# Attention outputs finished two steps later, weight preparation by a table of steps, a fourth word tile, one low part on VectorE

## The chip, the cores and the metric

The kernel runs on one core of a Trainium2 chip. The metric is the device time of one execution in microseconds (us), the median of several runs. Engines are named as in the profile: PE is TensorE (PEld its weight loads), DVE is VectorE, ACT is ScalarE, POOL is GpSimd, SP is SyncE, which issues DMAs.

## The reference

Three blocks follow one another, all on float32 data with 2 batches, 8 heads, 768 positions, head size 64 (model width 512).

```
# 1. attention inside clusters
q_assign = argmax(q_n @ c_n.T); k_assign = argmax(k_n @ c_n.T)       # 16 centroids per head
scores = where(q_assign == k_assign, (q @ k.T) / sqrt(D), -1e9)
attn = exp(scores - max); attn = attn / (sum(attn) + 1e-9)
x = attn @ v                                                          # heads side by side: (2, 768, 512)
# 2. mixing over positions, then a feed-forward block of width 2048
u = x + (xt @ U @ V).transpose;  y = u + relu(u @ w_ch1) @ w_ch2
# 3. gated block of width 1024
h = relu(y @ w_in); conv_out = 3-tap convolution of h along the positions
out = (h * sigmoid(conv_out)) @ w_out
```

## The kernel before, in words

Attention runs as 96 steps n, one for each head and each 128 of its 768 query rows, six to a head. Two heads make a pair, so a pair has twelve steps s = 0 to 11, and there are eight pairs (0 to 7). The whole program is written out by hand (`manual_schedule`): each engine executes its instructions in the order in which the code issues them, and waits only for data and for buffers. So the order of the calls in `step(n)` is the order of the work.

A step n issues, in this order: on PE the scores of step n + 2 (`s_mm`, tile `sc`, L356 and L367); in some steps other PE work; then six transposes of the exponentials of step n (`t_mm`, tile `tr`, L393, two tiles of three transposes). The copies of `tr` out of PSUM (tile `pt`, L400) follow one step later: the first half on ACT, the second on DVE. ACT forms the exponentials (L384), DVE scales the scores and takes their extreme (`s_max`, L373). When six rows of a head are transposed, `pv_mm` (L409) multiplies by the values in two lots of six matmuls, in steps of rest 2 and 5 of `g, r = divmod(n - 7, 6)`; these are s = 3, 9 and s = 6, 0. After the second lot ACT copies the sum (`asb`, L418); `fin_t` (L425, tile `at`) transposes it on PE in three matmuls, and `fin_x` takes the reciprocal of the sums (L431) and multiplies (L434, tile `x`) on DVE.

The PSUM pool `ps_t` has three tiles for `tr`, `at`, `sim`, `simw`, `oht`, `mt`, `mx`, so a transpose has to wait until one of the older three has been read out.

Beside this stand three kinds of work, put into fixed steps:
- the cluster masks of the next pair: `sims_wide` (s = 0), `sims_turn` (s = 2, tile `sim`, L224), five DVE operations ending in L249 (tile `oh`), `onehot_t` (tile `oht`, L263) and its rows on ACT (L269);
- the low parts of the next pair's operands, `split_ops` (L119, L120 on POOL, tile `ab`), in `prep(n)`;
- the preparation of weights. They come as 64-bit words and are joined to float32 by a chain of stages: DMA (`job_dma`, tile `raw`), `job_base` (ACT, L462), `job_low` (DVE, L470), `job_join` (DVE, L475), `job_put` and `job_more` (cast on ACT, low part on POOL). During attention `pump()` moves one job by one stage in every odd step; from step 86 on `begin()` and `tick()` take over, and the jobs still under way go on from there, one stage in a tick. The words stand in tiles `wx`, of which there are three (`word_tile`).

The mixing of a batch (`mix_t`, tile `mt`, L650; `mix_x`, tile `mx`, L670) is queued at s = 8 of the pair behind the batch's last and taken up in steps 3, 4, 9, 10 that issue no `fin_t`.

The feed-forward block (about 250 to 510 us of the span) forms seven products in place of eight with tiles pa to pd (L838), and sums (`acc`, L898 to L900) that DVE adds to `xa` (L902). The gated block has its own units (c, b, f): PE forms `g` (L930 to L932), ACT and DVE the convolution and gate (L933, L949, L953, L957, L959), and `split(f)` the high part (ACT, L963) and the low part (POOL, L964) of the product, which PE reads for `po` (L982).

Of the kernel before, what the change touches and what calls it, by code (L numbers as in the profile page):

```python
# [19 lines left out]
I32 = mybir.dt.int32  # L20
# [6 lines left out]
P = 128  # L27
# [6 lines left out]
def tile_kernel(ctx: ExitStack, tc: tile.TileContext, qk, vv, cen, u_w, v_w, w1, w2, win, wout, conv, out):  # L34
    nc = tc.nc
    B, H, D, _, S = qk.shape
    NC = cen.shape[0] // H
    NP = H // 2
# [18 lines left out]
    wst = right.enter_context(tc.tile_pool(name="wst", bufs=1, side="right"))  # L57
# [144 lines left out]
    ohst = {}  # L202
# [48 lines left out]
    def behind_onehot(b, p):  # L251

        seen = a_oh.tile([P, 1], BF16, tag="seen", name="seen")
        nc.gpsimd.tensor_copy(seen, kept[b, p][:, 0, 0:1])

    kept = {}

# [163 lines left out]
    def fin_t(g):  # L421
        asb = st.pop(("asb", g))
        pt = ps_t.tile([P, NK, 2, D], F32, tag="t", name="at")
        for t in range(NK):
            nc.tensor.transpose(pt[:, t].rearrange("p a d -> p (a d)"), asb[:, t * P:(t + 1) * P], identf)  # L425
        st["at", g] = pt
# [23 lines left out]
    def job_dma(j):  # L450
        raw_ = wst.tile([P, UN, 2], I32, tag="raw", name="raw", bufs=2)
        for p0, src in j["src"]:
            pn, n = src.shape
            nc.sync.dma_start(out=raw_[p0:p0 + pn, 0:n], in_=src.bitcast(I32).rearrange("p (a b) -> p a b", b=2))
        j["raw"] = raw_[0:p0 + pn, 0:n]
# [6 lines left out]
        nc.scalar.activation(j["b"], j["raw"][:, :, 1].bitcast(F32), AF.Prelu, scale=float(2.0 ** -112), alpha=float(2.0 ** 32))  # L462

    def word_tile():
        return wst.tile([P, UN], I32, tag="wx", name="wx", bufs=3)

    def job_low(j):
        pn, n, _ = j["raw"].shape
# [17 lines left out]
    def job_more(j, count=3):  # L486
        for f in j["left"][:count]:
            f()
        del j["left"][:count]
        if not j["left"]:  # L490
            del full[:j.get("held", 1)]

    THIN = {0: job_dma, 2: job_base, 3: job_low, 4: job_join, 5: job_put, 6: job_more, 8: job_more}

    def pump():

        for j in list(fly):
            j["at"] += 1
            if j["at"] in THIN:
                THIN[j["at"]](j)  # L500
            if j.get("left") == []:
                fly.remove(j)
        if jobs and not fly:
            j = jobs.pop(0)
            j["at"] = 0
            job_dma(j)
            fly.append(j)


    words, puts = [], []  # L510
# [11 lines left out]
    def tick():  # L522
        clock[0] += 1
        for j in fly:
            words.extend([lambda f=THIN[k], j=j: f(j) for k in sorted(THIN) if k > j["at"] and k < 6])
        fly.clear()
        if puts and puts[0][0] in opened:
            puts.pop(0)[1]()
        if words:
            words.pop(0)()  # L530
        elif begun and clock[0] - begun[0]["at"] > 4 and len(full) < 3:
            j = begun[0]
            job_base(j)

            def low():
                job_low(j)
                begun.pop(0)
                begin()

            def last():  # L540
                job_join(j)
                full.append(j)
                x = j["x"].bitcast(F32)
                steps = j["steps"](x) if "steps" in j else [lambda: j["put"](x)]
                for i, f in enumerate(steps):
                    puts.append((j["slot"], lambda f=f, i=i: (f(), full.pop(0) if i >= len(steps) - j["held"] else None)))

            words.extend([low, lambda: None, last])
# [138 lines left out]
    def prep(n):  # L687

        pair, s = divmod(n, 2 * NT)
        nxt = pair + 1  # L690
        if nxt < B * NP:
            b, p = divmod(nxt, NP)
            for part, at in enumerate(ONEHOT_AT[nxt == 1]):
                if s == at:
                    sims_onehot(b, p, part)
            if s == 1 and nxt == 2:
                load_ops(b, p, 0)
            if s == (1, 3)[nxt < 3]:
                split_ops(b, p, 0, nc.gpsimd)
            if s == (3, 1)[nxt == 1]:  # L700
                load_ops(b, p, 1)
            if s == 7:
                behind_onehot(b, p)
                split_ops(b, p, 1, nc.gpsimd)
        if s == RAW_AT[pair == 0] and pair + 2 < B * NP:
            load_raw(*divmod(pair + 2, NP))
        if s == V_AT[pair == 0] and nxt < B * NP:
            load_v(*divmod(nxt, NP))
        if s == 10 and 0 < pair < B * NP - 2:
            load_ops(*divmod(pair + 2, NP), 0)  # L710
        if n >= NQ - 10:
            begin()
            tick()
        elif n % 2 == 1 and n > 1:
            pump()


    PLAN = ({2: (0, 1, 2), 5: (3, 4, 5)}, NT - 1), ({0: (0, 1, 2), 1: (3, 4, 5)}, 1)
# [5 lines left out]
    def step(n):  # L724
        pair, s = divmod(n, 2 * NT)
        mix = None
        if s == 8 and pair > 0 and n < NQ:
            b, p = divmod(pair - 1, NP)
            if p == NP - 1:
                mixing.append(mix_t(b))  # L730
                mix_rest(b)
        if n == 0:
            sims_wide(0, 1)
            warm(7)
        if n + 2 < NQ:
            s_mm(n + 2)
        ahead = divmod(pair + 1, NP)
        wide = 0 <= n < NQ and 1 < pair + 1 < B * NP
        rows = 0 <= n < NQ and pair + 1 < B * NP and s == ROWS_AT[pair == 0]
        turn = 0 <= n < NQ and pair + 1 < B * NP and s == TURN_AT[pair == 0]  # L740
        if rows:
            onehot_t(*ahead)

        g, r = divmod(n - NT - 1, NT)
        ks, last = PLAN[g == NHEAD - 1]
        if 0 <= g < NHEAD:
            for k in ks.get(r, ()):
                pv_mm(g, k)
        done = g - 1 if r == 0 else g if g == NHEAD - 1 and r == last + 1 else -1
        if 0 <= done < NHEAD - (r == 0):  # L750
            fin_t(done)
        elif mixing and (s in MIX_AT or pair == B * NP - 1):
            mix = mixing.pop(0)
            got = mix[0]()
        if s == SIM_AT and wide:
            sims_wide(*ahead)
        if turn:
            sims_turn(*ahead)
        if 0 <= n < NQ:
            t_mm(n)  # L760
        soon = n + 1 >= NQ - 1
        if soon and n + 1 < NQ:
            s_exp(n + 1)
        if 0 <= n - 1 < NQ:
            for i in range(2):
                t_out(n - 1, i)
        if 0 <= n + 1 < NQ and not soon:
            s_exp(n + 1)
        if rows:
            onehot_rows(*ahead)  # L770
        if (s == SIM_AT and wide) or n == 0:
            sims_copy(*ahead)
        if n == -1:
            split_first(1, "q")
            split_ops(0, 0, 1, nc.gpsimd)
            load_ops(0, 1, 0)
        if n + 2 < NQ:
            s_max(n + 2)
        if 0 <= g < NHEAD and r == 0:
            sm = st["sum", g]  # L780
            nc.gpsimd.tensor_scalar(out=sm, in0=sm, scalar1=1e-9, scalar2=None, op0=ALU.add)
        if 0 <= g < NHEAD and r == last:
            fin_a(g)
        if 0 <= done < NHEAD - (r == 0):
            fin_x(done)
        if mix:
            mix[1](got)
        if 0 <= n < NQ:
            prep(n)
# [146 lines left out]
    def gate(c, b):  # L936

        h = hs[c, b]
        i = made[0] * 4
        made[0] = (made[0] + 1) % (len(spare_tiles) // 4)  # L940
        own = [x.rearrange("p k s -> p (k s)") for x in spare_tiles[i:i + 4]]
        hs[c, b] = [own[0:2], own[2:4]]
        cv = {}

        def conv(f, t):
            w = cw[:, FPC * c + f]
            x = cv[f, t] = ps_a.tile([P, DM], F32, tag="abcd"[2 * f + t], name="cv")[:, 0:HS]
            a, z = t * HS, (t + 1) * HS
            nc.scalar.activation(x, h[f][:, a:z], AF.Identity, scale=w[:, 1:2])  # L949
            for k, d in ((0, -1), (2, 1)):  # L950
                lo, hi = max(a, -d), min(z, S - d)
                o = x[:, lo - a:hi - a]
                nc.vector.scalar_tensor_tensor(out=o, in0=h[f][:, lo + d:hi + d], scalar=w[:, k:k + 1], in1=o, op0=ALU.mult, op1=ALU.add)  # L953

        def close(f, t):
            x = cv.pop((f, t))
            nc.scalar.activation(x, x, AF.Sigmoid)  # L957
            o = h[f][:, t * HS:(t + 1) * HS]
            nc.vector.tensor_mul(o, o, x)  # L959

        def split(f):
            gh, gl = hs[c, b][f]
            nc.scalar.copy(gh, h[f])  # L963
            nc.gpsimd.tensor_sub(gl, h[f], gh)  # L964

        todo = [(conv, 0, 0), (conv, 0, 1), (conv, 1, 0), (close, 0, 0), (conv, 1, 1), (close, 0, 1), (close, 1, 0), (close, 1, 1), (split, 0), (split, 1)]
        for part, *at in todo:
            part(*at)
            yield
# [292 lines left out]
```

## Time and profile before

| | |
|---|---|
| median of 3 runs | 640.44 us (640.26 to 640.55) |
| the profiled execution's own time | 640.48 us |
| its span, first to last instruction | 638.7 us |
| granted TensorE clock | 1.000 |
| PE busy | 629.0 us (98%) |
| DVE busy | 422.9 us (66%) |
| ACT busy | 370.2 us (58%) |
| POOL busy | 314.6 us (49%) |
| chain that ended last: PE | 88% |
| chain: DVE, ACT, POOL | 3%, 3%, 2% |

The span lies inside the execution's own time; 1.8 us lie around it. Busy time of PE counts a matmul from its start to its modelled end. A matmul that stands alone or is held back is drawn longer than one in a full stream, so a high busy share does not say that PE was never held up; the starts of successive groups say more.

### The profile page before, as it was taken

The page shows a single profiled execution, that of the slowest core. Times are in us where ns is not written, and L with a number is a line of the kernel's source. Part 1 is how long each engine was busy: PE and PEld are TensorE (multiplying, and loading weights), DVE is VectorE, ACT ScalarE, POOL GpSimd, SP SyncE. Part 2 cuts the span into 40 slices and gives each one's busy share as a digit, 9 for nine tenths or more (in the row PEclk, how much of TensorE's full clock was granted, in tenths as well). Part 3 has the DMA queues.
Part 4 walks back from the last instruction along what each step waited for, and adds up shares of the span by engine and source line. Part 5 has one row for each costly group of instructions (what it writes and reads, how often), then busy time and mean ns, then how long its engine had stood idle before and what let it go on. Part 6 is the DMA issues. An engine that isn't in the chain of part 4 may idle for free.

```text
span 638.7 us, 10486 instructions
## 1 busy us (share of the span) xinstructions
PE 629.0 (98%) x3850; PEld 548.1 (86%) x3850; DVE 422.9 (66%) x833; ACT 370.2 (58%) x752; POOL 314.6 (49%) x320
## 2 busy tenths in 40 slices
PE   8999999999999999999999999999999999999997
PEld 5767777766777767999999999999999998889986
DVE  6968788686868684586765666666666468641762
ACT  5967777776777674647363434343354498655730
POOL 4835445256346622878655545463355455413330
PEclk9999999999999999999999999999999999999999
DMA  7696764836445110112321221121112211200022
GB/s 192 139 210 152 142 164 85 182 74 170 81 114 123 60 56 29 35 39 94 107 93 66 90 77 66 67 67 67 66 47 75 79 34 67 66 1 2 4 96 99
DMA packets 17860, 55.50 MB, mean 87 GB/s; under 512 B 3120, under 2 KB 3760, under 8 KB 17808
## 3 DMA queue, kind: packets, MB, share of 16 engines
q1 hardware_dynamic: 14208, 40.08, 20.7%
q0 software_dynamic: 3600, 14.75, 11.2%
q8 instruction: 30, 0.49, 0.3%
q14 instruction: 22, 0.18, 0.1%
HBM read 50.19 MB, written 3.15 MB: 84 GB/s over the span
## 4 chain that ended last, share of the span: by engine, by line
PE 88%; DVE 3%; ACT 3%; POOL 2%; issue 2%; DMA 1%; ACTq 0%; DVEq 0%; POOLq 0%
PE po L982 10%; PE pv L409 10%; PE tr L393 9%; PE acc L898 7%; PE acc L900 7%; PE acc L899 7%; PE pd L838 5%; PE pa L838 5%; PE pb L838 5%; PE sc L367 5%; PE sc L356 5%; PE pc L838 2%; PE g L931 2%; PE g L930 2%; PE g L932 2%
## 5 line engine op out<-in xcount | busy, mean ns | idle before, releaser
L384 ACT ACTIVATE e<-e,nb 128x768 f32<-128x768 f32 x96 | 90.5, 943 | 20.7 <-DVE e L373 20.4
L373 DVE TENSOR_SCALAR_CACHE_REDUCE e<-sc 128x768 f32<-128x768 f32 x96 | 91.3, 952 | 8.3 <-PE sc L367 7.1
L902 DVE TENSOR_TENSOR xa<-acc,xa 128x384 f32<-128x384 f32 x128 | 70.2, 555 | 39.1 <-PE acc L900 39.1
L898 PE MATMUL acc<-r,vh 128*128 128x384 f32 x256 | 86.0, 336 | 0.4 <-DVE xa L902 0.4
L900 PE MATMUL acc<-r,vl 128*128 128x384 f32 x256 | 85.6, 334 | 0.0
L899 PE MATMUL acc<-r,vh 128*128 128x384 f32 x256 | 85.5, 334 | 0.0
L393 PE MATMUL tr<-identf,e 128*128 128x128 f32 x576 | 82.8, 277 | 2.3 <-DVE pt L400 1.7
L393 PEld LDWEIGHTS tr<-identf,e 128*128 128x128 f32 x576 | 64.9, 140 | 23.4 <-issue 8.7
L400 DVE COPY pt<-tr 128x384 f32<-128x384 f32 x93 | 51.4, 552 | 35.3 <-PE tr L393 34.9
L409 PE MATMUL pv<-pt,rv 128*64 128x384 f32 x384 | 69.3, 494 | 0.0
L601 POOL TENSOR_TENSOR vl<-wx,vh 128x512 fp32r<-128x512 f32 x24 | 30.8, 1299 | 63.4 <-ACT vh L600 63.4
L356 PE MATMUL sc<-ab 128*128 128x384 f32 x192 | 57.1, 378 | 0.4 <-DVE ab L192 0.3
L400 ACT COPY pt<-tr 128x384 f32<-128x384 f32 x99 | 47.2, 481 | 16.5 <-PE tr L393 16.1
L953 DVE SCALAR_TENSOR_TENSOR cv<-h,cw,cv 128x383 f32<-128x383 f32 (+1 forms) x64 | 38.2, 620 | 27.5 <-ACT cv L949 26.4
L409 PEld LDWEIGHTS pv<-pt,rv 128*64 128x64 f32 x384 | 26.2, 136 | 28.1 <-issue 24.8
L367 PE MATMUL sc<-cd 80*128 80x384 f32 x192 | 49.4, 339 | 0.0
L898 PEld LDWEIGHTS acc<-r,vh 128*128 128x128 f32 x256 | 48.0, 188 | 1.5 <-DVE xa L902 1.3
L899 PEld LDWEIGHTS acc<-r,vh 128*128 128x128 f32 x256 | 48.1, 188 | 0.0
L900 PEld LDWEIGHTS acc<-r,vl 128*128 128x128 f32 x256 | 48.0, 188 | 0.0
L475 DVE SCALAR_TENSOR_TENSOR wx<-wb,wy 128x512 int32<-128x512 int32 (+1 forms) x42 | 28.1, 669 | 22.8 <-POOL vl L601 12.4
L881 POOL TENSOR_TENSOR r<-q,r 128x384 fp32r<-128x384 f32 x16 | 16.2, 1015 | 49.9 <-ACT r L880 49.9
L575 POOL TENSOR_TENSOR wl<-wx,wh 128x512 fp32r<-128x512 f32 (+1 forms) x32 | 36.3, 1155 | 6.7 <-DVE oh L249 4.3
(242 smaller groups left out, 1532.3 us busy)
## 6 DMA issues: line engine op xcount, KB each, us to landing
raw<-in_w_dram SPq DMA_DIRECT2D x32, 512.0 KB, 3.6
cd<-in_qk_dram POOLq DMA_DIRECT2D x15, 384.0 KB, 4.2
ab<-in_qk_dram POOLq DMA_DIRECT2D x15, 384.0 KB, 5.4
raw<-in_win_dram SPq DMA_DIRECT2D x8, 512.0 KB, 3.6
raw<-in_wout_dram SPq DMA_DIRECT2D x8, 512.0 KB, 3.5
rv<-in_vv_dram SPq DMA_DIRECT2D x8, 384.0 KB, 3.4
out_dram<-xa SPq DMA_DIRECT2D x12, 256.0 KB, 2.0
ab<-in_qk_dram POOLq DMA_DIRECT2D x15, 192.0 KB, 5.5
```

The lines of the kernel that those rows point to most:

```text
L356: nc.tensor.matmul(ps[:, f, 0:HS], ab[:, 0, c0:c0 + P], ab[:, 1, f * HS:(f + 1) * HS], start=True, stop=False)
L367: nc.tensor.matmul(ps[:, f, 0:HS], cd[0:80, 0, c0:c0 + P], cd[0:80, 1, f * HS:(f + 1) * HS], start=False, stop=True)
L373: nc.vector.tensor_scalar(out=e, in0=ps[:, :, 0:HS], scalar1=-SCALE, scalar2=3e38, op0=ALU.mult, op1=ALU.min, accum_out=nb,)
L384: nc.scalar.activation(e, e, AF.Exp, scale=-1.0, bias=nb, accum_out=st["sum", n // NT][:, n % NT:n % NT + 1])
L393: nc.tensor.transpose(pt[:, k, :], e[:, i, k * P:(k + 1) * P], identf)
L400: (nc.scalar.copy if i == 0 or n in (2, 3, 4) else nc.vector.tensor_copy)(to, st.pop(("t", n, i)))
L409: nc.tensor.matmul(acc[i * D:(i + 1) * D], vts[b, h // 2][:, h % 2, k], pt[:, k, i * NK:(i + 1) * NK].rearrange("p a b -> p (a b)"), start ...
L838: nc.tensor.matmul(o, l[:, k, w], r[:, k], start=first and not more, stop=last, skip_group_check=more)
L898: nc.tensor.matmul(acc, wh[:, f, ds_], r[:, 0], start=f == t, stop=False)
L899: nc.tensor.matmul(acc, wh[:, f, ds_], r[:, 1], start=False, stop=False)
L900: nc.tensor.matmul(acc, wl[:, f, ds_], r[:, 0], start=False, stop=f != t)
L902: nc.vector.tensor_add(o, acc, o)
```

## The change

Four things change.

1. `fin_t` and `fin_x` of a head move from the step of rest 0 (s = 1 and 7) to that of rest 2 (s = 3 and 9). `fin_t` stands there ahead of the first lot of `pv_mm`. The last head keeps its own place. The mixing is queued at s = 10 rather than 8 and may share a step with `fin_t`.
2. `pump(s)` is called in every step and follows the table PARTS: DMA at s = 4, base at 9, low at 11, join at 0, put at 3, further parts at 5 and 8. A job so takes about a pair's twelve steps. `tick()` starts at step 87 rather than 86, and a job that is under way hands over what is left of its parts too.
3. There are four word tiles rather than three. In the first pair, the splits of the second pair's first head wait for that pair's mask: `behind_onehot` issues a one-column copy of `oh` on POOL (tile `seen`) ahead of them, at s = 5 rather than 3.
4. The low part of one unit of the gated block, (c, b, f) = (1, 0, 0), is formed by DVE rather than POOL (L964).

```diff
@@ -251,7 +251,7 @@
     def behind_onehot(b, p):
 
         seen = a_oh.tile([P, 1], BF16, tag="seen", name="seen")
-        nc.gpsimd.tensor_copy(seen, kept[b, p][:, 0, 0:1])
+        nc.gpsimd.tensor_copy(seen, (kept.get((b, p)) or ohst[b, p]["oh"])[:, 0, 0:1])
 
     kept = {}
 
@@ -462,7 +462,7 @@
         nc.scalar.activation(j["b"], j["raw"][:, :, 1].bitcast(F32), AF.Prelu, scale=float(2.0 ** -112), alpha=float(2.0 ** 32))
 
     def word_tile():
-        return wst.tile([P, UN], I32, tag="wx", name="wx", bufs=3)
+        return wst.tile([P, UN], I32, tag="wx", name="wx", bufs=4)
 
     def job_low(j):
         pn, n, _ = j["raw"].shape
@@ -492,19 +492,21 @@
 
     THIN = {0: job_dma, 2: job_base, 3: job_low, 4: job_join, 5: job_put, 6: job_more, 8: job_more}
 
-    def pump():
-
+
+    PARTS = {4: 0, 9: 2, 11: 3, 0: 4, 3: 5, 5: 6, 8: 8}
+    order = sorted(THIN)
+
+    def pump(s):
+        if s in PARTS and PARTS[s] == 0 and jobs:
+            fly.append(jobs.pop(0))
+            fly[-1]["at"] = -1
         for j in list(fly):
-            j["at"] += 1
-            if j["at"] in THIN:
-                THIN[j["at"]](j)
-            if j.get("left") == []:
+            k = order[order.index(j["at"]) + 1] if j["at"] >= 0 else 0
+            if PARTS.get(s) == k:
+                j["at"] = k
+                THIN[k](j)
+            if j.get("left") == [] or j["at"] == order[-1]:
                 fly.remove(j)
-        if jobs and not fly:
-            j = jobs.pop(0)
-            j["at"] = 0
-            job_dma(j)
-            fly.append(j)
 
 
     words, puts = [], []
@@ -523,6 +525,7 @@
         clock[0] += 1
         for j in fly:
             words.extend([lambda f=THIN[k], j=j: f(j) for k in sorted(THIN) if k > j["at"] and k < 6])
+            words.append(lambda j=j: j["left"] and job_more(j, 9))
         fly.clear()
         if puts and puts[0][0] in opened:
             puts.pop(0)[1]()
@@ -695,7 +698,9 @@
                     sims_onehot(b, p, part)
             if s == 1 and nxt == 2:
                 load_ops(b, p, 0)
-            if s == (1, 3)[nxt < 3]:
+            if s == (1, 3, 5)[(nxt < 3) + (nxt == 1)]:
+                if nxt == 1:
+                    behind_onehot(b, p)
                 split_ops(b, p, 0, nc.gpsimd)
             if s == (3, 1)[nxt == 1]:
                 load_ops(b, p, 1)
@@ -708,11 +713,11 @@
             load_v(*divmod(nxt, NP))
         if s == 10 and 0 < pair < B * NP - 2:
             load_ops(*divmod(pair + 2, NP), 0)
-        if n >= NQ - 10:
+        if n >= NQ - 9:
             begin()
             tick()
-        elif n % 2 == 1 and n > 1:
-            pump()
+        else:
+            pump(s)
 
 
     PLAN = ({2: (0, 1, 2), 5: (3, 4, 5)}, NT - 1), ({0: (0, 1, 2), 1: (3, 4, 5)}, 1)
@@ -724,7 +729,7 @@
     def step(n):
         pair, s = divmod(n, 2 * NT)
         mix = None
-        if s == 8 and pair > 0 and n < NQ:
+        if s == 10 and pair > 0 and n < NQ:
             b, p = divmod(pair - 1, NP)
             if p == NP - 1:
                 mixing.append(mix_t(b))
@@ -743,13 +748,17 @@
 
         g, r = divmod(n - NT - 1, NT)
         ks, last = PLAN[g == NHEAD - 1]
+        done = g - 1 if r == (2, 0)[g == NHEAD - 1] else g if g == NHEAD - 1 and r == last + 1 else -1
+        if 0 <= done and r:
+            fin_t(done)
         if 0 <= g < NHEAD:
             for k in ks.get(r, ()):
                 pv_mm(g, k)
-        done = g - 1 if r == 0 else g if g == NHEAD - 1 and r == last + 1 else -1
-        if 0 <= done < NHEAD - (r == 0):
+        if 0 <= done and r:
+            pass
+        elif 0 <= done:
             fin_t(done)
-        elif mixing and (s in MIX_AT or pair == B * NP - 1):
+        if mixing and (s in MIX_AT or pair == B * NP - 1 and not (0 <= done)):
             mix = mixing.pop(0)
             got = mix[0]()
         if s == SIM_AT and wide:
@@ -781,7 +790,7 @@
             nc.gpsimd.tensor_scalar(out=sm, in0=sm, scalar1=1e-9, scalar2=None, op0=ALU.add)
         if 0 <= g < NHEAD and r == last:
             fin_a(g)
-        if 0 <= done < NHEAD - (r == 0):
+        if 0 <= done:
             fin_x(done)
         if mix:
             mix[1](got)
@@ -961,7 +970,7 @@
         def split(f):
             gh, gl = hs[c, b][f]
             nc.scalar.copy(gh, h[f])
-            nc.gpsimd.tensor_sub(gl, h[f], gh)
+            (nc.vector if (c, b, f) == (1, 0, 0) else nc.gpsimd).tensor_sub(gl, h[f], gh)
 
         todo = [(conv, 0, 0), (conv, 0, 1), (conv, 1, 0), (close, 0, 0), (conv, 1, 1), (close, 0, 1), (close, 1, 0), (close, 1, 1), (split, 0), (split, 1)]
         for part, *at in todo:
```

How the instructions move on three engines. First PE in the second pair, steps s = 1 to 3, before:

```order
L393 MATMUL tr<-identf,e 128x128 x6
L356 MATMUL sc<-ab 128x384 x2
L367 MATMUL sc<-cd 128x384 x2
L425 MATMUL at<-identf,asb 128x128 x3
L393 MATMUL tr<-identf,e 128x128 x6
L356 MATMUL sc<-ab 128x384 x2
L367 MATMUL sc<-cd 128x384 x2
L224 MATMUL sim<-identf,sw 128x128 x3
L393 MATMUL tr<-identf,e 128x128 x6
L356 MATMUL sc<-ab 128x384 x2
L367 MATMUL sc<-cd 128x384 x2
L409 MATMUL pv<-pt,rv 64x384 x6
```

The same twelve places after the change:

```order
L393 MATMUL tr<-identf,e 128x128 x6
L356 MATMUL sc<-ab 128x384 x2
L367 MATMUL sc<-cd 128x384 x2
L393 MATMUL tr<-identf,e 128x128 x6
L356 MATMUL sc<-ab 128x384 x2
L367 MATMUL sc<-cd 128x384 x2
L224 MATMUL sim<-identf,sw 128x128 x3
L393 MATMUL tr<-identf,e 128x128 x6
L356 MATMUL sc<-ab 128x384 x2
L367 MATMUL sc<-cd 128x384 x2
L425 MATMUL at<-identf,asb 128x128 x3
L409 MATMUL pv<-pt,rv 64x384 x6
```

The three transposes `at` leave s = 1 and stand behind the scores of s = 3, ahead of `pv`; nothing else changes its place.

DVE in the fifth pair (pair 4), s = 1 to 3 before, with the first lot of words of a 128x512 weight block in it:

```order
L373 TENSOR_SCALAR e,nb<-sc 128x768
L431 RECIPROCAL rs<-sum 128x6
L434 TENSOR_TENSOR x<-at,rs 128x6x64
L470 TENSOR_SCALAR wx<-raw 128x512
L400 COPY pt<-tr 128x3x128
L373 TENSOR_SCALAR e,nb<-sc 128x768
L241 TENSOR_REDUCE mx<-sim 128x24
L400 COPY pt<-tr 128x3x128
L373 TENSOR_SCALAR e,nb<-sc 128x768
L243 TENSOR_TENSOR eq<-sim,mx 128x384
L245 TENSOR_TENSOR eq<-eq,iota 128x384
```

The stretch from the end of the fourth pair to s = 3 of the fifth after the change:

```order
L470 TENSOR_SCALAR wx<-raw 128x512
L400 COPY pt<-tr 128x3x128
L373 TENSOR_SCALAR e,nb<-sc 128x768
L475 SCALAR_TENSOR_TENSOR wx<-wb,wx 128x512
L400 COPY pt<-tr 128x3x128
L373 TENSOR_SCALAR e,nb<-sc 128x768
L400 COPY pt<-tr 128x3x128
L373 TENSOR_SCALAR e,nb<-sc 128x768
L241 TENSOR_REDUCE mx<-sim 128x24
L400 COPY pt<-tr 128x3x128
L373 TENSOR_SCALAR e,nb<-sc 128x768
L431 RECIPROCAL rs<-sum 128x6
```

The stage `wx<-raw` has moved three steps up, to s = 11 of the pair before, `wx<-wb,wx` to s = 0, and the reciprocal has moved behind the `s_max` of s = 3.

POOL in the first pair, before:

```order
L119 TENSOR_TENSOR ab<-rq,cd 64x768
L120 TENSOR_TENSOR ab<-rk,ab 64x768
L781 TENSOR_SCALAR sum<-sum 128x6
L254 COPY seen<-oh 128x1
L119 TENSOR_TENSOR ab<-rk,cd 64x768
L120 TENSOR_TENSOR ab<-rq,ab 64x768
```

and after the change:

```order
L254 COPY seen<-oh 128x1
L119 TENSOR_TENSOR ab<-rq,cd 64x768
L120 TENSOR_TENSOR ab<-rk,ab 64x768
L790 TENSOR_SCALAR sum<-sum 128x6
L254 COPY seen<-oh 128x1
L119 TENSOR_TENSOR ab<-rk,cd 64x768
L120 TENSOR_TENSOR ab<-rq,ab 64x768
```

The copy `seen`, which reads the finished mask, now stands ahead of the first two splits as well.

## Rows read from the trace of the kernel before

**Rows 1.** Page, part 1: busy time of each engine, share of the span, instructions.

```profile
PE 629.0 (98%) x3850; PEld 548.1 (86%) x3850; DVE 422.9 (66%) x833; ACT 370.2 (58%) x752; POOL 314.6 (49%) x320
```

**Rows 2.** Waits of PE: line, what for, us in total, times, longest.

```profile
PE tr L393 <- DVE pt L400: 1.7, 2, 1.3
...
PE po L982 <- ACT h L933: 0.5, 1, 0.5
...
PE tr L393 <- ACT os L269: 0.2, 1, 0.2
```

**Rows 3.** Timeline of PE: start, us, line; pair 1, s = 7, 8; pair 2, s = 2.

```profile
57.08 0.82 PE L393 MATMUL tr<-identf,e 128*128 128x128 f32 x6
57.65 0.59 PE L356 MATMUL sc<-ab 128*128 128x384 f32 x2
...
58.43 0.93 PE L393 MATMUL tr<-identf,e 128*128 128x128 f32 x6
...
59.12 0.60 PE L356 MATMUL sc<-ab 128*128 128x384 f32 x2
...
72.66 1.01 PE L393 MATMUL tr<-identf,e 128*128 128x128 f32 x6
...
73.43 0.60 PE L356 MATMUL sc<-ab 128*128 128x384 f32 x2
```

**Rows 4.** Timeline of DVE and PE in the third pair, s = 2, 3.

```profile
72.05 0.56 DVE L434 TENSOR_TENSOR x<-at,rs 128x384 f32<-128x384 f32 x1
...
72.52 0.55 DVE L400 COPY pt<-tr 128x384 f32<-128x384 f32 x1
...
72.98 0.95 DVE L373 TENSOR_SCALAR_CACHE_REDUCE e<-sc 128x768 f32<-128x768 f32 x1
...
74.30 2.16 PE L409 MATMUL pv<-pt,rv 128*64 128x384 f32 x12
```

**Rows 5.** Timeline: words and splits in the fourth pair (first row) and fifth.

```profile
104.19 0.42 DVE L470 TENSOR_SCALAR wx<-raw 128x512 int32<-128x512 int32 x1
...
127.20 1.82 POOL L120 TENSOR_TENSOR ab<-rk,ab 64x768 fp32r<-64x768 f32 x1
...
127.85 1.45 DVE L470 TENSOR_SCALAR wx<-raw 128x512 int32<-128x512 int32 x1
...
127.99 0.31 PEld L393 LDWEIGHTS tr<-identf,e 128*128 128x128 f32 x3
...
130.13 0.60 PE L356 MATMUL sc<-ab 128*128 128x384 f32 x2
```

**Rows 6.** Timeline of PE in the eighth pair, s = 2.

```profile
204.19 0.49 PE L393 MATMUL tr<-identf,e 128*128 128x128 f32 x3
...
205.22 0.59 PE L356 MATMUL sc<-ab 128*128 128x384 f32 x2
```

**Rows 7.** Timeline: the first pair's mask (three rows), and the third's (last).

```profile
25.14 1.82 POOL L119 TENSOR_TENSOR ab<-rq,cd 64x768 fp32r<-64x768 f32 x1 [1.20 <-DMA cd<-in_qk_dram]
...
25.43 1.94 DVE L249 TENSOR_TENSOR oh<-eq,m 128x384 bf16<-128x384 bf16 x1
...
27.89 0.50 PE L263 MATMUL oht<-identb,oh 128*64 128x128 bf16 x6 [0.57 <-DVE pt L400]
...
79.62 0.56 DVE L249 TENSOR_TENSOR oh<-eq,m 128x384 bf16<-128x384 bf16 x1
```

**Rows 8.** Timeline of DVE and PE in the feed-forward block.

```profile
301.42 0.69 DVE L475 SCALAR_TENSOR_TENSOR wx<-wb,wy 128x512 int32<-128x512 int32 x1 [1.75 <-POOL wl L575]
...
302.63 0.44 PE L898 MATMUL acc<-r,vh 128*128 128x384 f32 x1 [0.43 <-DVE xa L902]
```

**Rows 9.** Timeline: a DVE subtraction (first), and the gated block.

```profile
237.88 0.95 DVE L802 TENSOR_TENSOR u0T3l<-x,u0T3h 128x768 fp32r<-128x768 f32 x1
...
530.52 1.85 POOL L964 TENSOR_TENSOR u0T4l<-h,u0T4h 128x768 fp32r<-128x768 f32 x1 [5.92 <-ACT u0T4h L963]
...
532.41 0.49 ACT L933 ACTIVATE h<-g 128x384 f32<-128x384 f32 x1 [0.43 <-POOL u0T4l L964]
```

## Prediction

> **What bounds the kernel now.** The busy times come first: PE has 629.0 us in a span of 638.7, DVE 422.9, POOL 314.6 [rows 1]. So the time is PE's work plus whatever holds PE up. The change keeps every PE instruction and only sets some elsewhere, and the granted clock is 1.000 throughout, so the whole question is which waits of PE go and which come. The second view is the waits of PE, and it lists little: 1.7 us of transposes behind DVE's copies, 0.5 of `po`, 0.2 behind `os` [rows 2], and single ones of 0.57 and 0.43 that come below. The third view is the starts in PE's timeline, because a wait that falls inside a drawn matmul is no gap. The reader should lay a step of attention beside its neighbour: from the six `tr` to the next `sc` it is 57.65 - 57.08 = 0.57 us in s = 7, but 59.12 - 58.43 = 0.69 in s = 8, and 73.43 - 72.66 = 0.77 in s = 2 [rows 3]. That is the same work; the rest is a stall without a gap. Why there: the transposes need a PSUM tile that DVE reads out, and before that copy DVE has the multiplication `x`, 72.05 to 72.61, inside a step without `pv` [rows 4]. In such a step PE goes on quickly; in one with `pv` it is 2.16 us longer on the way [rows 4].
>
> **Outputs two steps later (first edit).** Removed are `at`, the reciprocal and `x` from s = 1 and 7; they come back in s = 3 and 9 with the same durations. On PE `at` is worth the same wherever it stands, zero. What goes is the hold-up in the following step:
> - s = 8: 0.69 - 0.57 = 0.12 us in seven pairs, 0.8 us.
> - s = 2: 0.77 - 0.57 = 0.20 in the five plain pairs 1, 2, 3, 5, 6, 1.0 us.
> - s = 2 of pair 7: the first three `tr` start at 204.19, `sc` at 205.22 [rows 6], 1.03 us for 0.57, so 0.46.
> - s = 2 of pair 4: from 127.99 to 130.13 [rows 5], 2.14 us for 0.57, so 1.57. Here the second edit has to help, next paragraph.
>
> What is late next in s = 3? DVE has the copy of `tr`, the scaling, the reciprocal and `x`. The scaling takes 0.95 and `x` 0.56 [rows 4], with the short reciprocal between them; PE has three `at` (half of 0.57) and 2.16 of `pv` before a transpose needs that tile. So `x` is ready by roughly 1.8 of 2.4 us behind the scores, a margin of 0.6: hidden. If that cover is gone, the price is what `x` lacks, twice a pair.
>
> **Weights by the table (second edit).** No operation is added, but each meets other neighbours. The shift of a 128x512 block of words on DVE takes 0.42 us at 104.19 and 1.45 at 127.85, where POOL's split runs from 127.20 to 129.02 [rows 5]. That stands directly before the copy for which the transposes wait (the 1.3 us in rows 2). In the new order it is at s = 11 and the join at s = 0, and POOL's splits are at s = 1 and 7. I take the 1.57 as gone. The bound on the other side: the same 1.03 us of stretching comes back at s = 11 in the four pairs with blocks of that size, ahead of `pv` and `simw` of s = 0; that would be hidden behind 2.16 us, so at most 0 to 1. The steps of rest that a pump brings to SP and POOL are one DMA per pair as before; the only two rows that change places on SP are a load of values and one of words, and both have more than a step to land.
>
> On this the Trainium skill speaks (SBUF — State Buffer, "Who interferes with whom"): VectorE's copies and scalar operations in their two-port modes, and its operations with two SBUF inputs, share a port pair with GpSimd, and the one that comes second blocks fully until the first is done. At 127.85 this fits only roughly: the shift ended at 129.30, 0.28 after the split's end, less than its own 0.42. The rule also speaks against the change: at s = 3 the table now sets POOL's put beside the mask's operations on two SBUF operands, and by it each such meeting would cost all that POOL has left to do. This is the third rival, with its price from rows.
>
> **First pair (third edit).** Before, the split starts at 25.14 and L249, which writes the mask, takes 1.94 us beside it against 0.56 in the third pair [rows 7]. DVE is then 1.4 us behind, and PE waits three times: 0.57 at `oht` [rows 7], 1.7 - 1.3 = 0.4 at `tr`, 0.2 behind `os` [rows 2], 1.2 us in sum. A group that waits also loses its overlap with the one before (`tr` is drawn 0.82 long but `sc` begins after 0.57, rows 3: 0.25 us); I add two of these three, 0.5, so 1.7. The splits now begin behind the mask, a little before 26.2, and end about 30; the operand is first needed in step 10, some 4 us later. Hidden. The split and the second one then follow each other closely; if POOL were late, step 10 or 16 would wait, and nothing in the rows says so.
>
> **Fourth word tile.** DVE's join waits 1.75 us for POOL to read out a tile, starts at 301.42, and behind it stands the addition for which PE waits 0.43 [rows 8]. With a fourth tile the join starts when its words are there, and the wait of PE goes: 0.43 and 0.2 of overlap, 0.6.
>
> **Gate unit on DVE.** POOL's subtraction runs 530.52 to 532.37, and ACT has waited 0.43 us for it when L933 starts at 532.41 [rows 9]; that L933 is at the head of the chain of ACT work before the `po` that waits 0.5 [rows 2]. A DVE subtraction of 128x768 takes 0.95 at 237.88 [rows 9], 0.9 less, but two products stand ahead of it on DVE. The gain is between 0 (DVE late, or stretched beside POOL's next subtraction, which could now start earlier) and 0.43 (then ACT's own cast limits it); I take 0.33, that is DVE done at about 532.05. DVE's join behind it comes 0.95 later and has some 3 us until its cast.
>
> **New costs.** Three places are not in the rows of before: `mx` and `at` in one step in pairs 5 and 6, four times; a shift and a join more, of 0.69 each [rows 8], among the additions at the start of the feed-forward block, as the jobs under way are handed over one step later; and the mixing two steps later beside ACT's and POOL's other work. From below they are 0 each, and a little under it where they leave another place; from above 4 x 0.2 (the stall of s = 2) plus 0.4 (the stall at 302.63), 1.2 in all. Each has a cover, so I take 0.5, nearer to 0 than to 1.2.
>
> **Sum.** 0.8 + 1.0 + 0.46 + 1.57 = 3.8 for the outputs and the shift; 1.7 first pair; 0.6 tile; 0.33 gate: 6.5. Less 0.5 makes 6.0. The profiled execution took 640.48 us, 1.8 more than its span, which I leave as it is: 634.5. The median is 0.04 under that execution, so 634.4.
>
> **Rivals.**
> 1. *The hidden stalls move along.* DVE has 0.55 + 0.95 = 1.5 us for copy and scaling [rows 4] in a plain step, which is 58.43 - 57.08 = 1.35 us on PE [rows 3], so DVE is behind anyway, and what it is spared in s = 2 and 8 is lost in another step. Then only what the waits list goes: 1.7 (rows 2) + 0.57 + 0.2 + 0.43 + 0.33 = 3.2, less 0.5: 637.7. For it: several small stalls are at the end of a run of steps without `pv`. Against: the step s = 7 shows 0.57 with a full DVE.
> 2. *Slower: `at` ahead of `pv` waits.* `at` needs a PSUM tile whose last reader is ACT's or DVE's copy of a step before. PE executes in order, so `pv`, `tr` and the scores stand behind it, in 15 heads. In s = 9 it is DVE's copy, issued behind the scaling of the step before; in before the last such copy ends about when the scores do. If it came 0.55 late (one copy, rows 4), 15 x 0.55 = 8.3 us would be lost, 642.7; from 0.5 us per head upward the kernel is slower than before by more than a measurement can tell. Against: DVE is rid of 0.75 us of `x` just before s = 9.
> 3. *POOL's put meets the mask.* In pairs 5 and 6 POOL now starts the low parts of a block in s = 3 and 4, where L249 stands. At 1.4 us as in rows 7, twice, with `oht` two steps later, at most 2.8: 637.2; with the slack of a `pv` step between them more likely half of it.
> 4. *The change does little,* because the wait at 127.99 comes from the order of PSUM tiles and not from the shift. Without its 1.57 and with rival 1: 639.3 to 640.5, no change.
>
> **Chances and range.** Forecast 0.70 (632.8 to 636); rival 1 0.11; rival 3 0.07; rival 4 0.06; rival 2 0.06. A measurement here can tell 0.2%, 1.3 us, from no change, so faster means under 639.1: the forecast and rivals 1 and 3, 0.88; the same 0.06; slower 0.06. The range takes in, below, the first pair and tile with all their overlap and no new costs (another 1.5 us, so 632.8) and above rivals 1 and 3: 632.6 to 638.2.
>
> **What would show it.** Right: `tr` to `sc` of about 0.57 in s = 2 and 8 of all pairs; a shift of 0.42 to 0.7 and no gap of PE in pair 4; L249 at 0.56 in the first pair with no wait at `oht`; no wait of `acc` near 302; L933 some 0.3 earlier against the scores before it, and `po`'s wait near 0.2. Wrong: waits of `at` in s = 3 or 9 or of `tr` behind `x` there; `oht` waiting in pairs 5 and 6; PE's waits in the feed-forward block longer than before. If the time is under 632.5, stalls that I counted at nothing went as well; over 638, the stalls of attention only changed their step.

## The result and the profile after

The changed kernel takes 634.55 us (median of 6 runs, 634.04 to 635.69) against 640.39 us (6 runs, 640.04 to 640.64), a ratio of 0.9912 with an interval of 0.9899 to 0.9925. That is 5.84 us less; 6.0 was forecast, 634.4 us. The profiled execution took 634.59 us, its span 632.8 against 638.7.

Page of the changed kernel, part 1 and the first line of the chain:

```profile
PE 626.6 (99%) x3850; PEld 550.0 (87%) x3850; DVE 423.8 (67%) x834; ACT 368.7 (58%) x752; POOL 313.0 (49%) x320
...
PE 94%; DVE 2%; ACT 2%; issue 1%; POOL 0%; ACTq 0%; DVEq 0%
```

Against [rows 1], PE's instructions are the same in number, and every engine is about as busy as before. Only the chain has moved, from 88% on PE to 94%: waits have gone, not work. The waits of PE after the change (line, what for, us in total, times, longest) are the whole list (late lines have numbers up to nine higher than before):

```profile
PE idle L147 <- DVE busy L142: 1.1, 1, 1.1
PE oht L313 <- DVE oh L249: 0.3, 1, 0.3
PE sc L356 <- DVE ab L192: 0.2, 1, 0.2
PE tr L393 <- ACT pt L400: 0.2, 1, 0.2
PE tr L393 <- DVE tt L662: 0.2, 1, 0.2
PE po L991 <- ACT h L942: 0.2, 1, 0.2
```

Of [rows 2], the 1.7 us behind DVE's copies and the 0.2 behind `os` are gone, and `po` has 0.2 of its 0.5 left. The stalls without a gap need the timeline of PE (start, us, line). Pair 1, s = 7 and 8, and below them pair 2, s = 2:

```profile
55.98 0.82 PE L393 MATMUL tr<-identf,e 128*128 128x128 f32 x6
56.56 0.59 PE L356 MATMUL sc<-ab 128*128 128x384 f32 x2
...
57.34 0.82 PE L393 MATMUL tr<-identf,e 128*128 128x128 f32 x6
57.91 0.59 PE L356 MATMUL sc<-ab 128*128 128x384 f32 x2
...
71.41 0.82 PE L393 MATMUL tr<-identf,e 128*128 128x128 f32 x6
71.98 0.60 PE L356 MATMUL sc<-ab 128*128 128x384 f32 x2
```

From `tr` to `sc` it is 0.58, 0.57 and 0.57 us, where [rows 3] had 0.57, 0.69 and 0.77. The six transposes of these steps are all drawn 0.82 long, too: the 0.93 and 1.01 of before were the stall, inside the drawn matmuls.

For a full account I set the starts of PE's groups of both profiles side by side, step by step, and counted where the distance between them changes (`at` counted with the place that it moved to):

| place | before to after, us | forecast |
|---|---|---|
| s = 2 of pairs 1 to 7 | -0.24, -0.26, -0.24, -1.63, -0.25, -0.25, -0.10 | |
| s = 8 of pairs 1 to 7 | -0.12, -0.11, -0.12, -0.11, -0.09, -0.45, -0.10 | |
| both together | -4.07 | -3.8 |
| first pair, mask | -1.40 | -1.7 |
| additions near 302 us (fourth tile) | -0.69 | -0.6 |
| `po` near 536 us (gate unit) | -0.34 | -0.33 |
| end of attention, near 237 us | -0.27 | 0 |
| products near 343 us | -0.15 | 0 |
| mixing (s = 9, 10 of pair 4, and the steps of `mx`) | +0.06 | part of +0.5 |
| other small steps of attention | +0.10 | part of +0.5 |
| first 11 us, before any of the changed code | +0.81 | 0 |

These add up to -5.95; the spans differ by 5.9. The last row is no effect of the change. Idle matmuls (on one constant tile; nothing uses their result) and the first products stand there, in the same order in both programs, but this execution went through them later. Four idle matmuls and PE's first scores, before and then after:

```profile
4.87 0.81 PE L147 MATMUL idle<-busy 128*128 128x384 bf16 x4
...
9.90 1.23 PE L356 MATMUL sc<-ab 128*128 128x384 f32 x4 [0.32 <-DVE ab L192]
```

```profile
5.15 1.49 PE L147 MATMUL idle<-busy 128*128 128x384 bf16 x4
...
10.71 1.23 PE L356 MATMUL sc<-ab 128*128 128x384 f32 x4 [0.23 <-DVE ab L192]
```

The same four matmuls take 0.81 and 1.49 us: before, PE's clock had risen by then, and after the change it had not. The last section follows this through all profiles.

In the ten profiles of the experiments the first scores start between 9.87 and 11.36 us. So medians of a few runs carry some tenths from there, and the places of a profile tell small effects apart better.

### The profile page after: what moved, and what is told of

Same layout as the page of the kernel before. It is cut to its first block, busy times and chain, and to the rows that moved or that the text cites. A ratio compares the mean times of both kernels' runs of the same rounds, so it can differ in the third digit from the quotient of the medians.

```text
span 632.8 us, 10482 instructions
## 1 busy us (share of the span) xinstructions
PE 626.6 (99%) x3850; PEld 550.0 (87%) x3850; DVE 423.8 (67%) x834; ACT 368.7 (58%) x752; POOL 313.0 (49%) x320
## 4 chain that ended last, share of the span: by engine, by line
PE 94%; DVE 2%; ACT 2%; issue 1%; POOL 0%; ACTq 0%; DVEq 0%
PE tr L393 11%; PE pv L409 10%; PE po L991 10%; PE acc L907 7%; PE acc L909 7%; PE acc L908 7%; PE pa L847 5%; PE pd L847 5%; PE pb L847 5%; PE sc L367 5%; PE sc L356 5%; PE pc L847 3%; PE g L941 2%; PE g L940 2%; PE g L939 2%; PE idle L147 1%
## 5 line engine op out<-in xcount | busy, mean ns | idle before, releaser
L393 PE MATMUL tr<-identf,e 128*128 128x128 f32 x576 | 80.7, 276 | 0.5 <-ACT pt L400 0.2
L400 DVE COPY pt<-tr 128x384 f32<-128x384 f32 x93 | 51.5, 554 | 33.4 <-PE tr L393 33.0
L400 ACT COPY pt<-tr 128x384 f32<-128x384 f32 x99 | 47.0, 479 | 18.6 <-PE tr L393 18.5
L475 DVE SCALAR_TENSOR_TENSOR wx<-wb,wy 128x512 int32<-128x512 int32 (+1 forms) x43 | 28.7, 668 | 17.7 <-ACT wb L462 17.3
```

What stands on the lines that cost most here:

```text
L393: nc.tensor.transpose(pt[:, k, :], e[:, i, k * P:(k + 1) * P], identf)
L400: (nc.scalar.copy if i == 0 or n in (2, 3, 4) else nc.vector.tensor_copy)(to, st.pop(("t", n, i)))
```

## The experiments

All runs are compared with the changed kernel's 634.55 us and, place by place, with its profile. First, one part undone at a time.

**Outputs back in s = 1 and 7.**

```diff
-        done = g - 1 if r == (2, 0)[g == NHEAD - 1] else g if g == NHEAD - 1 and r == last + 1 else -1
+        done = g - 1 if r == 0 else g if g == NHEAD - 1 and r == last + 1 else -1
...
```

Left out are three conditions that then keep the last head in its place.

> The changed kernel, but fin_t and fin_x back in s = 1 and 7; table, tiles, split and gate unit as changed. Theory (the multiplication x in a step without pv holds up the copy that the transposes wait for; at pair 4 it needs the stretched shift as well): s = 2 loses about 0.25 in six pairs, pair 4 among them, s = 8 about 0.11 in six and 0.45 in pair 6: 2.6 us, so 637.1. First rival (outputs alone make the stall of pair 4): 1.6 there, 638.5. Second rival (the stalls only move to another step): 634.5 to 635.

Measured: 637.29 us (636.57 to 637.53). In every pair s = 2 loses 0.24 or 0.25, pair 4 included (pair 7: 0.10), and s = 8 loses 0.09 to 0.12, in pair 4 0.46; the end of attention loses 0.27 at one group of transposes and regains 0.08 at the next. Pair 2, s = 2, with DVE's work in front of it:

```profile
71.31 0.56 DVE L434 TENSOR_TENSOR x<-at,rs 128x384 f32<-128x384 f32 x1
...
71.79 0.55 DVE L400 COPY pt<-tr 128x384 f32<-128x384 f32 x1
71.93 1.01 PE L393 MATMUL tr<-identf,e 128*128 128x128 f32 x6
...
72.69 0.59 PE L356 MATMUL sc<-ab 128*128 128x384 f32 x2
```

0.76 us from `tr` to `sc`, as in [rows 3], and `x` stands before the copy, as in [rows 4]. The theory holds, and the second rival is out: these stalls don't move on, they come and go with the place of `x`. The first rival is out as well, since pair 4 loses only 0.25 without the stretched shift.

**The old pump.**

```diff
-        if n >= NQ - 9:
+        if n >= NQ - 10:
...
-        else:
+        elif n > 1:
             pump(s)
```

Left out is the body of `pump`, which is again that of before: one stage in every odd step. The outputs stay late.

> The changed kernel, but a job moves by one stage in every odd step as before and tick starts at step 86; outputs stay late. Theory: in pair 4 the shift again runs beside POOL's split and takes about 1.45 us, but x is not ahead of it, so 0.75 of it is hidden and PE loses about 0.8 there: 635.4. First rival (the stretched shift alone makes the stall): 1.6, 636.2. Second rival (the table does nothing): 634.5, the shift 0.42.

Measured: 635.65 us (635.47 to 635.96). The five largest losses are 0.63 at s = 2 of pair 4, 0.41 at s = 9 of pair 1 (there `at` waits 0.2), 0.20 and 0.21 at s = 2 of pairs 3 and 6, and 0.22 at the end of attention. Pair 4, POOL's split, the shift and the transposes:

```profile
124.12 1.83 POOL L120 TENSOR_TENSOR ab<-rk,ab 64x768 fp32r<-64x768 f32 x1 [0.35 <-DMA rk<-in_qk_dram]
...
125.34 0.89 DVE L470 TENSOR_SCALAR wx<-raw 128x512 int32<-128x512 int32 x1
...
126.75 0.55 PE L393 MATMUL tr<-identf,e 128*128 128x128 f32 x3 [0.41 <-DVE pt L400]
```

The shift is stretched again, but begins late in the split and has no `x` in front of it, so 0.63 is left of 1.63. A pump that does nothing is out. The sizes are not those of the theory: the shift took 0.89 and not 1.45, and at its places this run loses about 1.7 us and not 0.8; the time came near 635.4 because its first scores were 0.84 us earlier than in the changed kernel's profile.

**Outputs late alone, on the kernel before.** The edit is that of `done`, of the order of `fin_t`, `pv_mm` and mixing in `step`, and of the step that queues the mixing, as in the change, and nothing else.

> The kernel before with the outputs finished two steps later, and nothing else (pump, tiles, split and gate unit as before). Theory: s = 2 gives back 0.25 in five pairs and s = 8 0.1 in six, pair 4 about 1.0 of its 1.6, since the shift beside the split still takes 1.45, pair 6 its 0.45 or less: 3.0 us, so 637.5. Rival (without the table the stalls move to s = 3 and 9): 639.5 or more, with transposes that wait there.

Measured: 638.27 us (637.70 to 638.97), ratio to before 0.9962 (0.9947 to 0.9977). Its profile is 1.2 us behind in its first steps, where the granted clock fell to 0.50 from 8.82 to 12.23 us; counted from there it gains 3.0 in attention, the sum of the theory, though not by its parts. s = 8 gains the full amounts; pair 4 gives 1.24 of its 1.63; but pair 1 loses 0.36 and pairs 3 and 6 keep their 0.2, the same three places as with the old pump. Of the rival only that 0.36 is seen, at s = 9. In pair 4 the gain is not that of the outputs alone, because POOL's split began earlier against PE than in [rows 5] and the shift was stretched to 0.65 only:

```profile
126.43 1.84 POOL L120 TENSOR_TENSOR ab<-rk,ab 64x768 fp32r<-64x768 f32 x1 [0.43 <-DMA rk<-in_qk_dram]
...
127.90 0.65 DVE L470 TENSOR_SCALAR wx<-raw 128x512 int32<-128x512 int32 x1
...
129.07 0.55 PE L393 MATMUL tr<-identf,e 128*128 128x128 f32 x3 [0.17 <-DVE pt L400]
```

So a shift of 0.65 without `x` ahead of it costs PE 0.39, one of 0.89 (the old pump) 0.63: all but 0.26 of it. By these two, one of 1.45 would cost 1.2 (an estimate; no run had it), so most of pair 4's 1.63 is the stretched shift, and the table alone gives back 1.38 (the run with early outputs).

**Early split in the first pair.**

```diff
-            if s == (1, 3, 5)[(nxt < 3) + (nxt == 1)]:
-                if nxt == 1:
-                    behind_onehot(b, p)
+            if s == (1, 3)[nxt < 3]:
```

> The changed kernel, but the splits of the second pair's first head at s = 3 of the first pair without the copy seen ahead of them. Theory: L249 takes about 1.9 us beside POOL's split and oht, tr and tr wait again: 1.4 us more, 636.0. Rival (DVE catches up, since the outputs no longer stand there): L249 1.9 but under 0.4 us of waits, 634.9.

Measured: 635.27 us (635.20 to 635.78), in its profile 1.54 us more in the first pair (the first scores were 0.7 us earlier than in the changed kernel's profile, which is why the time shows only half). The mask's last operation and PE:

```profile
25.38 1.83 POOL L119 TENSOR_TENSOR ab<-rq,cd 64x768 fp32r<-64x768 f32 x1 [1.34 <-DMA cd<-in_qk_dram]
25.53 2.09 DVE L249 TENSOR_TENSOR oh<-eq,m 128x384 bf16<-128x384 bf16 x1
...
28.14 0.49 PE L263 MATMUL oht<-identb,oh 128*64 128x128 bf16 x6 [0.73 <-DVE pt L400]
```

and in the changed kernel:

```profile
26.26 0.55 DVE L249 TENSOR_TENSOR oh<-eq,m 128x384 bf16<-128x384 bf16 x1
...
26.96 0.19 POOL L254 COPY seen<-oh 128x1 bf16<-128x1 bf16 x1 [2.21 <-DVE oh L249]
27.10 1.82 POOL L119 TENSOR_TENSOR ab<-rq,cd 64x768 fp32r<-64x768 f32 x1
```

By its places the theory holds; the rival's 0.4 us of waits is out.

**Three word tiles.** `bufs=4` becomes `bufs=3`.

> The changed kernel with three word tiles. Theory: in the feed-forward block one join on DVE waits some 1.7 us for POOL to read out a tile, and PE's additions wait 0.4 behind it, 0.6 to 0.7 us from start to start: 635.2. Rival (the jobs now run at other times, so three tiles would do): no wait of a join, 634.5.

Measured: 635.21 us (635.06 to 635.32). DVE's join and PE's addition:

```profile
296.49 0.69 DVE L475 SCALAR_TENSOR_TENSOR wx<-wb,wy 128x512 int32<-128x512 int32 x1 [1.73 <-POOL wl L578]
...
297.70 0.45 PE L907 MATMUL acc<-r,vh 128*128 128x384 f32 x1 [0.41 <-DVE xa L911]
```

The wait of [rows 8] is back as it was, and this is the only place behind attention that differs: 0.69 us. The theory holds. (The time also holds 0.37 us lost in the second pair, see below, and first scores 0.52 us earlier than in the changed kernel's profile.)

**The gate unit's low part on POOL.** `nc.gpsimd` in that one place.

> The changed kernel with the one low part back on POOL. Theory: L933 of that unit waits 0.4 us for POOL and po 0.5 instead of 0.16, 0.34 us from start to start: 634.9. Rival (ACT's own queue sets the time of po, whoever forms the low part): po as in the changed kernel, 634.5.

Measured: 634.53 us (633.94 to 634.93), no difference in time. The time is that of the rival; but the profile differs from the changed kernel's in one place behind attention, by 0.34 us, as the theory says:

```profile
526.83 0.49 ACT L942 ACTIVATE h<-g 128x384 f32<-128x384 f32 x1 [0.45 <-POOL u0T4l L973]
...
530.34 0.50 PE L991 MATMUL po<-vh,u 128*128 128x512 f32 x1 [0.50 <-ACT h L942]
```

The trace shows the term; the time of single runs can't, as the first 11 us alone vary by more.

Then a version that goes on from the change, where its waits list still names the mixing (`tr` behind `tt`).

**The mixing tile read out whole.** For the first batch, ACT and DVE read the 128x128 tile once each; POOL sets the pieces in place.

```diff
+            if b == 0:
...
+                nc.scalar.copy(hi, pt)
+                nc.vector.tensor_sub(lo, pt, hi)
+                for c in range(ND):
...
+                    nc.gpsimd.tensor_copy(tts[b][0:R, cs], hi[c * R:(c + 1) * R])
+                    nc.gpsimd.tensor_copy(tts[b][R:2 * R, cs], lo[c * R:(c + 1) * R])
+                nc.gpsimd.tensor_copy(tts[b][2 * R:3 * R], tts[b][0:R])
+                return
```

> The changed kernel, but the first batch's mixing tile is read out whole: one cast on ACT and one subtraction on DVE of 128x128 in place of four each of 32x128; nine copies on POOL then set the pieces in place. Theory (the 1.07 us on ACT and 1.19 on DVE hold up the copies behind them): the 0.8 us that PE loses at 147 to 149 shrinks to under 0.2, 633.9. Rival (POOL's copies hold up its DMAs and the next split, and the first mx waits): 634.6 or more, with a wait of mx or sc.

Measured: 633.35 us (633.04 to 633.80). The step behind the mixing gains 0.80, all of its loss, and neither `mx` nor a later `sc` waits, so the rival is out. But in pair 1, which the edit does not touch, PE lost 0.52:

```profile
47.05 1.82 POOL L120 TENSOR_TENSOR ab<-rk,ab 64x768 fp32r<-64x768 f32 x1 [0.27 <-POOL ab L119]
...
47.19 1.89 DVE L245 TENSOR_TENSOR eq<-eq,iota 128x384 bf16<-128x384 bf16 x1
...
51.90 0.44 PE L263 MATMUL oht<-identb,oh 128*64 128x128 bf16 x5 [0.45 <-ACT pt L400]
```

It is the collision of the first pair again, one pair later. There POOL's split starts when its DMA has landed, at 44.92 to 47.73 us in the profiles, so it depends on the execution whether it meets L245, which took 0.36 to 1.89 us there.

**The second pair's splits behind the mask too.** On top of the mixing tile read out whole:

```diff
-            if s == (1, 3, 5)[(nxt < 3) + (nxt == 1)]:
-                if nxt == 1:
+            if s == (1, 5)[nxt < 3]:
+                if nxt < 3:
```

> The changed kernel with the first batch's mixing tile read out whole (as in the run x1), and in the second pair too the splits wait for the mask, at s = 5 behind the copy seen. Theory (there POOL's split starts when a DMA lands, and where it meets L245 or L249 that takes 1.9 us and PE waits 0.5): both at about 0.4 and 0.56 in every execution, so 633.0 and the runs closer together. Rival (the operand comes too late then): scores wait at the start of the third pair, 633.5 or more.

Measured: 633.41 us (633.17 to 633.68): the rows as expected (L245 0.36, L249 0.56), but the time 633.0 was missed: it is not lower than without this edit. The rival's wait of scores is not in the trace. The changed kernel and this one were then run again, on one chip.

> The changed kernel once more, for a second profile. Theory (what differs between its executions lies at two places whose code the change left alone or only moved: the first 11 us, and the second pair, where POOL's split starts when a DMA lands): the first scores between 9.9 and 11.4 us, L245 of the second pair between 0.36 and 1.9 us, every other step within 0.05 us of the first profile; median 634.5. Rival (the spread comes from the feed-forward block): differences behind 250 us.

> The run x2 once more, beside the changed kernel on the same chip: the mixing tile read out whole and the second pair's splits behind the mask. Theory: 0.8 us from the mixing and a few tenths from the second pair in some executions, 1 us below the changed kernel, 633.4, with L245 and L249 of the second pair at 0.36 and 0.56. Rival (nothing in time): within 0.4 us of the changed kernel.

Measured: 634.41 us (633.88 to 634.53) for the changed kernel, 0.9901 (0.9887 to 0.9915) of before; 633.11 us (633.00 to 633.62) for the other, 0.9885 (0.9871 to 0.9899). The changed kernel's second profile differs from its first by -0.40 in the first 11 us and +0.19 in s = 0 of pair 1, where the wide products `simw` wait for data, and by nothing over 0.05 us in any other place; the spread does not come from the feed-forward block. L245 took 1.04 us there against 0.84, and PE lost nothing by it. The last version's mixing:

```profile
145.59 0.27 ACT L661 CAST mhi<-mt 128x128 fp32r<-128x128 f32 x1 [1.11 <-PE mt L653]
145.88 0.29 DVE L662 TENSOR_TENSOR mlo<-mt,mhi 128x128 fp32r<-128x128 f32 x1 [0.72 <-ACT mhi L661]
```

where the changed kernel has four casts and four subtractions:

```profile
146.31 1.07 ACT L660 CAST tt<-mt 32x128 fp32r<-32x128 f32 x4 [1.11 <-PE mt L653]
...
147.41 1.19 DVE L662 TENSOR_TENSOR tt<-mt,tt 32x128 fp32r<-32x128 f32 x4 [1.53 <-ACT tt L660]
```

It is the fastest of all, 1.3 us under the changed kernel measured beside it. In the two profiles 0.8 of it lie at the mixing; the rest lies in the first 11 us (0.30) and in s = 0 of pair 1 (0.22), the two places in which the changed kernel's own profiles differ. That the second pair's splits behind the mask gain time is not shown.

## Why the prediction was right

*The outputs.* The mechanism was right, and the sub-terms came where they were put: 0.1 at s = 8, 0.25 at s = 2 (0.20 was forecast). One label was wrong: the stall at 204.19 [rows 6] is s = 8 of pair 6, not s = 2 of pair 7, so its 0.46 was right and its cause only half: s = 2 of pair 7 gave 0.10, and the 0.46 comes back neither with early outputs under the table (0.09) nor with late outputs under the old pump (none). In that stall `x` itself begins 0.46 us after the reciprocal; with early outputs the same wait stands in s = 8 of pair 4 (0.46 lost). What `x` waits for there is open. That `x` in s = 3 is hidden behind `pv` is shown: no `tr` waits behind it, and with `at` counted there s = 3 and 9 are as long as before.

*The shift.* Its 1.57 went (1.63), but not because DVE's words no longer meet a split. In pair 4 the shift of s = 11 takes 0.42; the collision has moved to the join at s = 0:

```profile
119.84 0.42 DVE L470 TENSOR_SCALAR wx<-raw 128x512 int32<-128x512 int32 x1
...
121.36 1.81 POOL L119 TENSOR_TENSOR ab<-rq,cd 64x768 fp32r<-64x768 f32 x1 [3.09 <-DMA cd<-in_qk_dram]
121.52 2.20 DVE L475 SCALAR_TENSOR_TENSOR wx<-wb,wx 128x512 int32<-128x512 int32 x1
```

It costs DVE 1.5 us and PE nothing, as `pv` and `simw` of that step cover it. The prediction's upper bound had such a case for the shift itself, and that came too, one time: the shift at 179.03, two pairs later, takes 1.81 beside the split of 178.73, and there PE lost nothing either. So the cover carried this term, not the distance from the splits.

*First pair, tile, gate.* 1.40 for 1.7, 0.69 for 0.6, 0.34 for 0.33. In the first pair I had added 0.5 of lost overlap to 1.2 us of gaps, and 0.2 was there; undoing it costs 1.54, 0.14 more. DVE finished the gate's low part at 526.44, when ACT's own cast ended too, and L942 started at 526.53: the gain was at ACT's limit, which lies near 0.34 and not at the 0.43 of the prediction. Three rows of the changed kernel:

```profile
525.49 0.95 DVE L973 TENSOR_TENSOR u0T4l<-h,u0T4h 128x768 fp32r<-128x768 f32 x1
525.60 0.84 ACT L972 CAST u<-h 128x768 fp32r<-128x768 f32 x1 [0.30 <-DVE h L968]
...
526.53 0.49 ACT L942 ACTIVATE h<-g 128x384 f32<-128x384 f32 x1
```

*New costs.* The 0.5 was not found: 0.06 and 0.10. The mixing waits as long in its new place as in the old (0.8 us), so moving it neither gave nor took. `mx` beside `at`, and POOL's put at s = 3, cost nothing visible. On the other side 0.42 us near 237 and 343 us were gained that I had set at nothing. The first is mainly the table's: 0.22 comes back at the same transposes with the old pump, and late outputs alone give 0.05. Before, ACT runs `job_base` (L462) from 235.85 to 236.53, ahead of the copy (L400) for which these transposes wait; in the changed kernel the copy starts at 231.68 and L462 at 232.54. The 0.27 that early outputs lose is another stall, one group of transposes earlier. The 0.15 near 343 comes back in none of the runs that undo one part; its cause is open.

So the sum of 6.0 was 6.8 at its places and 5.95 with the late start of that execution. That the median came out 0.15 us from the forecast is luck: two errors of opposite sign, each under a microsecond, met. The late start is one that the prediction had ruled out when it read a clock of 1.000 throughout; that is the profile's mean, and in the first 4 to 7 us of every profile PE ran at half of it (last section).

*The rivals.* Stalls that move along: out by the first run. `at` ahead of `pv`: PE's waits list has no wait of `at`; with the old pump there was one of 0.2, in one head of 15. POOL's put against the mask: not seen, but its mechanism was, with the split in place of the put, in the second pair of some executions (0.52 and, with three tiles, 0.37 us). The change doing little: out.

## What to carry to other kernels

Lay equal steps beside each other by their starts: of the 4 us of stalls in attention the waits list showed less than half, the rest lay inside drawn matmuls. An operation of an engine that is not the bottleneck belongs into a step in which the bottleneck has long work of its own; here its collisions then cost nothing, although they went on. A start that a DMA sets can differ from profile to profile (by 2.8 us here), so put such work behind a fixed event if anything critical can meet it.

## What the runs showed of the hardware

These DVE operations, where they met a POOL subtraction that had begun, ended a fixed time after it, wherever they had started. L470 in the old pump: POOL until 125.95, DVE until 126.23, 0.28 later, alone 0.42. L245 in the run with the mixing tile read out whole: 48.87 and 49.08, 0.21, alone 0.36. L475 in the changed kernel: 123.17 and 123.72, 0.55, alone 0.68. L249 in [rows 7]: 26.96 and 27.37, 0.41, alone 0.56. Each time it is its own duration less 0.13 to 0.15. The Trainium skill (SBUF — State Buffer, "Who interferes with whom") says that the second to come is blocked until the first has ended, not slowed; these four cases agree, and the 0.28 that looked like a misfit in the prediction is that same rest. Copies of PSUM tiles (L400) beside the same splits kept their 0.55.

The first 11 us vary by up to 1.5 us between executions of the same instructions, and most of this is TensorE's clock. In all twelve profiles PE begins with the same idle matmuls at 1.12 us. They first start 0.32 us apart, which for 384 columns is the lower of the clock's two levels (1.2 GHz), and then 0.16 us apart, the upper one (2.4 GHz). The rise comes at 4.05 us in the profile of before and at 6.82 us in that of the changed kernel. In the ten profiles in which the clock then stays up, the first scores follow it: they start at 9.87 to 10.01 us where it rose before 5 us (five profiles), at 10.19 to 10.31 where it rose at 5.2 to 6.0 (three), and at 10.71 and 10.73 where it rose at 6.8. In the other two it rose at 5.2 and 5.4, but the granted clock fell to 0.50 again, from 8.64 to 12.05 us (outputs back in s = 1 and 7) and from 8.82 to 12.23 (outputs late alone), and the first scores start at 10.77 and 11.36; in the last one PE also waited 0.24 us for a DMA. What lets the clock rise earlier in one execution than in another is open.
